# A written order, separate load places and GpSimd steps for the w_k products of an attention, RWKV-FFN and conv-FFN kernel

## Chip, core and metric

The kernel runs on one core of a Trainium2 chip. The metric is the device time of one execution in microseconds (us), lower is better. TensorE does the matrix products, VectorE and ScalarE the element-wise work, GpSimd (POOL in the profile) some of it, and SyncE (SP) starts most DMA transfers.

## What is computed

The output of a causal attention is the input of a token-mixing feed-forward layer, whose output is the input of a second feed-forward layer with a convolution of three taps. The part that changes is the first half of the middle layer, `k = max(xk @ w_k, 0)` and the first of the six column slices of `k*k @ w_v`.

```python
x = attention(q, k, v)                      # (2, 448, 768), causal softmax, 12 heads of 64
x_prev = x shifted by one token
xk = mu_k * x + (1 - mu_k) * x_prev         # (896 tokens, 768)
xr = mu_r * x + (1 - mu_r) * x_prev
k = np.maximum(xk @ w_k, 0.0)               # w_k: 768 x 1024
v = k * k @ w_v                             # w_v: 1024 x 768
r = 1.0 / (1.0 + np.exp(-(xr @ w_r)))
x = r * v
h = np.maximum(x @ w_in, 0.0); gate = sigmoid(conv3(h, conv_w))
return (h * gate) @ w_out
```

## The kernel before

**Products.** Every matrix product runs in three passes: each float32 operand is kept as a high part H and a remainder L (both in the type that TensorE takes at full rate), and `mm3` issues H*H, H*L, L*H. For `xk @ w_k` the kernel uses a 2x2 scheme with seven block products instead of eight. Its eight columns of 128 are taken in four groups g = 0 to 3, each with one 128-column slice of the left half of w_k and one of the right half. Group g needs seven weight operands of 128x384: A11, A12, A22 are pieces of the two slices, S1 to S4 are sums and differences of pieces (step D). Each operand gets a step H (a copy to the product type) and a step L (the remainder). A product P1 to P7 is nine matmuls of 448 columns. P1, P6, P7, P4 add into one PSUM bank (A), P5 and P3 into another (B), P2 has its own (D), with evictions between: P1, P5, P6 are copied out (cp), P2, P3, P7 are added to a copy (ad), and the result goes through max with 0 (re), square (sq), H (kh) and L (kl) to become `k2[f]` for one half of the tokens. P4 ends its bank with re, sq, kh, kl. `k2[f]` is then the right operand of the w_v slices (`pv0` to `pv5` in the profile, 48 matmuls each).

**Weights.** Weights come as 8-byte floats. A load puts them in a place of 8-byte words; `narrow` makes 4-byte floats of them in place, step a on ScalarE and step e on VectorE. Two places (`raws`) are used in turn by all slices, so a load waits until all readers of the slice before the last are done. Prepared operands lie in four places (`whls`), of two operands each for w_k.

**Order.** The attention part before (`ORDER`, up to 122 us in the profile) and the last part (`LATE`) follow lists written out in the kernel: one token is one step, and each engine does its steps in the list's order. Between them, from `START = 3` on, the loops over `PORD` (products) and `WORDER` (operands) give program order, and the framework's scheduler sets each engine's order. Each engine works through its queue in order, so a step that waits holds all behind it. All VectorE and ScalarE steps of `k_split`, `k_out` and `k_evict` are on those two engines; GpSimd has nothing between 120 us and 280 us but one clearing of 0.1 us.

Of the kernel before, what the change touches and what calls it, by code (L numbers as in the profile page):

```python
# [22 lines left out]
def kernel(  # L23
# [629 lines left out]
    PORD = [(x, 0) for x in ("P1", "P2", "P5", "P6", "P3", "P7")]  # L653
    for g_ in range(1, KH):
        PORD += [(x, g_) for x in ("P1", "P5", "P2", "P6")] + [("P4", g_ - 1), ("P3", g_), ("P7", g_)]
    WORDER = [(n, 0) for n in ("A11", "A12", "S1", "S2", "S4", "S3", "A22")]
    WORDER += [(n, g_) for g_ in range(1, KH) for n in ("A11", "S1", "A12", "S2", "S4", "S3", "A22")]
    place = {w: n for n, w in enumerate(WORDER)}
    k_raw, w_pairs, w_done, k_bank, k_begun = {}, {}, {}, {}, set()

    def w_value(g_, n):
# [14 lines left out]
            split_l(eng or "v", t[:, 1], x, t[:, 0])  # L676

    def w_operand(g_, n):
        i, j = divmod(place[n, g_], 2)
        if i not in w_pairs:  # L680
            w_pairs[i] = whls.get(f"q{i}", f"wq{i}")[:, :, :2 * WT].rearrange("p a (b c) -> p a b c", b=2)
        return w_pairs[i][:, :, j]

    def k_product(x, g_):
        g_ = int(g_)
        a, b, acc = USES[x]
        more = (acc, g_) in k_begun
        if not more:
            k_begun.add((acc, g_))
            k_bank[acc, g_] = bank(f"k{acc}{g_}", 1) if pinned[0] else next_bank(f"k{acc}{g_}")  # L690
# [8 lines left out]
        n = place[a, g_]  # L699
        w_done[n // 2] = w_done.get(n // 2, 0) + 1  # L700
        if w_done[n // 2] == 2:
            whls.put(f"q{n // 2}")
# [93 lines left out]

    HALF = [slice(0, 512), slice(512, NT)]

    def token_mm(name, w, x, late_):
# [3 lines left out]
        order = [(c, b) for b in range(B) for c in KORD[:-2]] + [(c, b) for b in range(B) for c in KORD[-2:]] if late_ else [
            (c, b) for b in range(B) for c in range(n)]
        for i, (c, b) in enumerate(order):
            if k_tail and i == B * (n - 2):
                k_tail.pop()()
                for y in range(2):
                    whls.put(f"v{y}")
            products(out_[b], w, x, HALF[b], n, c, order[-1][0])  # L810
# [5 lines left out]
    def k_convert(g_):  # L816
        for r in range(2):
            if not loaded:
                load_next()
            raw, n, name = loaded.pop(0)[1]  # L820
            k_raw[g_, r] = raw
            convert(raw, n, name)

    def k_split(g_, n):
        if n[0] == "S":
            w_step(g_, n, "D", "")
        w_step(g_, n, "H", "s")
        w_step(g_, n, "L", "v")

    def k_out(a, f, b, relu):  # L830
        if k2[f] is None:
            k2[f] = big(f"Y{KHOME[f]}", f"k2_{f}")
        if relu:
            nc.scalar.activation(a, a, AF.Relu)
        nc.scalar.activation(a, a, AF.Square)
        split_h("s", k2[f][:, 0, TOK[b]], a)
        split_l("v", k2[f][:, 1, TOK[b]], a, k2[f][:, 0, TOK[b]])
# [428 lines left out]
```

## Time and profile before

| | us |
|---|---|
| median of three timed runs (lowest to highest) | 351.71 (351.44 to 353.42) |
| profiled execution, its own time | 353.43 |
| its span, first to last instruction | 351.6 |
| PE busy in the span | 338.7 |
| DVE (VectorE) busy | 275.2 |
| ACT (ScalarE) busy | 249.0 |
| POOL (GpSimd) busy | 93.1 |

TensorE's granted clock is 1.00 of full speed (2.4 GHz) over the whole span. A busy engine is executing an instruction; time between instructions is put down to what released the next one.

### The profile page before, as it was taken

What the parts mean: (1) busy time and instruction counts of PE and PEld (TensorE: products, weight loads), DVE (VectorE), ACT (ScalarE), POOL (GpSimd) and SP (SyncE); (2) the same over time, 40 slices, a digit from 0 to 9 for tenths busy, and PEclk for the clock granted to TensorE, in tenths of its full rate; (3) what the DMA queues carried; (4) which work ended last, traced back from release to release, by engine and by line L of the source; (5) the groups of instructions that cost most, each with busy time, mean ns of one, the idle gap of its engine ahead of it and who ended that gap; (6) DMA issues with size and microseconds to landing.
All of it is one profiled execution on the core that took longest, in us unless ns stands there. A gap on an engine that the chain in (4) does not pass through costs nothing.

```text
span 351.6 us, 7133 instructions
## 1 busy us (share of the span) xinstructions
PE 338.7 (96%) x2644; PEld 302.7 (86%) x2644; DVE 275.2 (78%) x604; ACT 249.0 (71%) x545; POOL 93.1 (26%) x153
## 2 busy tenths in 40 slices
PE   8989999999999999998979999999999999999995
PEld 7677788988898999897858999998988999999995
DVE  3999989999999949769566987446686889898731
ACT  2999989999880068889897875334657878766501
POOL 8376978866410400000000000000000000367110
PEclk9999999999999999999999999999999999999999
DMA  6658577251150052241793765222505200379623
GB/s 170 147 125 208 131 215 181 69 168 46 58 168 2 0 179 93 87 125 56 277 349 124 258 246 180 89 89 91 179 15 167 89 0 3 67 134 213 126 90 136
DMA packets 60095, 45.28 MB, mean 129 GB/s; under 512 B 31624, under 2 KB 58668, under 8 KB 60060
## 3 DMA queue, kind: packets, MB, share of 16 engines
q1 hardware_dynamic: 55916, 39.31, 36.7%
q0 software_dynamic: 3408, 5.33, 7.7%
q8 instruction: 21, 0.34, 0.4%
q10 hardware_dynamic: 736, 0.18, 0.2%
q14 instruction: 14, 0.11, 0.1%
HBM read 38.12 MB, written 2.75 MB: 116 GB/s over the span
## 4 chain that ended last, share of the span: by engine, by line
PE 67%; ACT 13%; DVE 11%; DMA 5%; issue 2%; SPq 1%; DVEq 0%; ACTq 0%
PE pv L69 16%; PE A L69 7%; PE po L425 5%; ACT p L377 5%; PE pr L69 4%; PE B L69 4%; PE c L69 2%; PE s L355 2%; ACT wt L138 2%; PE D L69 2%; DVE mixed L637 2%; DVE wq L94 2%; DMA wk6raw<-in_moe_w_k_dram 2%; PE W L600 2%; DVE xopX L94 1%
## 5 line engine op out<-in xcount | busy, mean ns | idle before, releaser
L1089 POOL DMA_DIRECT2D s<-g x12 | 12.6, 1169 | 131.4 <-ACT st L90 124.8
L377 ACT ACTIVATE p<-e,st 128x192 f32<-128x192 f32 (+6 forms) x84 | 42.4, 522 | 2.3 <-DVE st L368 2.2
L75 POOL TENSOR_SCALAR p<-p,st 128x256 f32<-128x256 f32 (+6 forms) x74 | 36.5, 512 | 16.3 <-DVE st L385 10.0
L368 DVE CUSTOM_DVE_ANT_0 e<-s,mask 128x192 f32<-128x192 f32 (+6 forms) x84 | 31.4, 413 | 1.8 <-PE s L355 1.6
L1006 DVE SCALAR_TENSOR_TENSOR cv<-hT,cw,cv 128x448 f32<-128x448 f32 x32 | 21.5, 680 | 6.7 <-ACT cv L1003 6.6
L425 PE MATMUL po<-pt,v 128*64 128x128 f32 (+4 forms) x384 | 24.1, 277 | 0.2 <-ACT pt L82 0.2
L425 PEld LDWEIGHTS po<-pt,v 128*64 128x64 f32 x384 | 20.2, 137 | 3.5 <-ACT pt L82 0.6
L355 PE MATMUL s<-kT,qT 64*64 64x192 f32 (+6 forms) x336 | 22.3, 385 | 0.6 <-ACT kT L82 0.5
L355 PEld LDWEIGHTS s<-kT,qT 64*64 64x64 f32 x336 | 14.7, 132 | 6.5 <-ACT kT L82 0.9
L377 ACT ACTIVATION_READ_ACCUMULATOR p<-e,st 128x1 f32 x84 | 17.7, 211 | 0.0
L69 PE MATMUL kA<-xopX,wq 128*128 128x448 f32 x72 | 16.7, 367 | 0.7 <-DVE aP L854 0.7
L846 ACT ACTIVATE aP<-kB 128x448 f32<-128x448 f32 x4 | 2.2, 543 | 21.4 <-PE kB L69 21.4
L69 PEld LDWEIGHTS kA<-xopX,wq 128*128 128x128 f32 x72 | 13.4, 188 | 2.2 <-DVE aP L854 1.1
L963 POOL MEMSET hT<- 128x6 f32 x1 | 0.1, 107 | 54.1 <-PE kA L69 54.1
L1012 DVE TENSOR_TENSOR cv<-cv,hT 128x448 f32<-128x448 f32 x16 | 9.9, 621 | 4.4 <-ACT cv L1010 4.3
L1010 ACT ACTIVATE cv<-cv 128x448 f32<-128x448 f32 x16 | 9.1, 568 | 5.6 <-DVE cv L1006 5.6
L69 PE MATMUL pv<-k,wv0hl 128*128 128x512 f32 (+1 forms) x48 | 10.2, 368 | 2.5 <-ACT wv0hl L90 2.2
L94 DVE TENSOR_TENSOR k<-aP,k 128x448 fp32r<-128x448 f32 x16 | 9.9, 620 | 3.5 <-ACT k L90 3.3
L94 POOL TENSOR_TENSOR xr<-m,xr 128x448 fp32r<-128x448 f32 x10 | 12.0, 1204 | 1.8 <-ACT xr L90 1.2
L69 PEld LDWEIGHTS pv<-k,wv0hl 128*128 128x128 f32 x48 | 8.6, 188 | 4.2 <-ACT wv0hl L90 2.6
L1201 ACT ACTIVATE o<-A 128x384 f32<-128x384 f32 x3 | 1.5, 491 | 14.5 <-PE A L69 14.5
L1003 ACT ACTIVATE cv<-hT,cw 128x448 f32<-128x448 f32 x16 | 10.7, 667 | 1.0 <-DVE g L94 0.8
(446 smaller groups left out, 1085.6 us busy)
## 6 DMA issues: line engine op xcount, KB each, us to landing
rqk<-in_q_dram SPq DMA_DIRECT2D x23, 112.0 KB, 3.2
v<-in_v_dram SPq DMA_DIRECT2D x24, 96.0 KB, 3.5
s<-g POOLq DMA_DIRECT2D x12, 192.0 KB, 3.8
rqk<-in_k_dram SPq DMA_DIRECT2D x16, 112.0 KB, 3.0
wo6raw<-g POOLq DMA_DIRECT2D x8, 192.0 KB, 4.7
wv0raw<-in_moe_w_v_dram SPq DMA_DIRECT2D x1, 1022.0 KB, 4.9
wv1raw<-in_moe_w_v_dram SPq DMA_DIRECT2D x1, 1022.0 KB, 7.2
wv2raw<-in_moe_w_v_dram SPq DMA_DIRECT2D x1, 1022.0 KB
```

Source lines behind the costliest of these rows:

```text
L69: nc.tensor.matmul(ps_out, x, y, start=first and i == 0, stop=last and i == 2, skip_group_check=more,)
L75: nc.gpsimd.tensor_scalar(out_, in_, s, 1.0, ALU.mult, ALU.mult)
L94: e.tensor_tensor(out_, x, f32(h), ALU.subtract)
L355: nc.tensor.matmul(held[self.name(f"s{f}")][1][h, o:z], qT[r, i * LO:(i + 1) * LO], kT[r, :(i + 1) * LO], start=True, stop=True,)
L368: nc.vector.tensor_tensor_reduce(t[:, :w], used(self.name(f"s{f}"))[:, o:z], mask[:, S - w:], -SCALE, 3e38, ALU.add, ALU.min, self.st[:, 0 ...
L377: nc.scalar.activation(p[:, :w], self.s[i][:, :w], AF.Exp, bias=self.st[:, 0, i:i + 1], scale=-1.0, accum_out=self.st[:, 1, i:i + 1],)
L425: nc.tensor.matmul(self.T["po"][j * D:(j + 1) * D, 1 + i * LO - z:1 + (i + n) * LO], self.v[:, kc, j], self.T["pt"][:, a - z:a + n * LO], ...
L1003: nc.scalar.activation(a, x[:, 0:S], AF.Copy, scale=cw[:, f:f + 1])
L1006: nc.vector.scalar_tensor_tensor(a, x[:, j:S + j], cw[:, j * NF + f:j * NF + f + 1], a, ALU.mult, ALU.add)
L1010: nc.scalar.activation(a, a, AF.Sigmoid)
L1012: (nc.gpsimd if eng == "p" else nc.vector).tensor_tensor(a, a, hc, ALU.mult)
L1089: nc.gpsimd.dma_start(out=dst, in_=f32(x), accum_op=ALU.add)
```

## The change

1. The loops over `PORD` and `WORDER` go. A list `PK` takes their place, in the manner of `ORDER`: it fixes the order of the seven products' remaining runs, of all operand steps, evictions and of the first w_v slice (tokens V0 to V7, one for each `k2[f]`) on TensorE, ScalarE, VectorE and GpSimd, and that of the loads.
2. The raw slices of group 2 (wk2, wk6) load into the places of `k2[2]` and `k2[6]`, outputs that are written later. The two `raws` places then serve groups 1 and 3 and the w_v slices.
3. The max with 0 of P2, P3 and P7 moves from ScalarE to GpSimd. So do step D of S3 and S4 and step L of A22 in groups 1 to 3, from VectorE.
4. The copies out of PSUM get two more places (five in all), and the last A22 operand a place of its own.
5. The last P4 stands after V0 and V4 in the list. The number of products and matmuls is the same.

A token reads `step.group:kind/engine`: `P2.1:ad` is the eviction `ad` of P2 in group 1, `S3.1:D/p` the difference S3 of group 1 on GpSimd, `k2.1:L` the load of group 2's second slice (`a` and `e` narrow it), `v0:h` a step of the first w_v slice, `P3.1` alone the product.

```diff
-    START = 3
-    w_next = len(WORDER) // KH
-    for n, (x, g_) in enumerate(PORD):
-        if n >= START:
-            k_product(x, str(g_))
-        k_evict(x, g_)
...
-            k_split(h, a)
-            w_next += 1
...
+    a_free = list(mslots.free) + list(
+        act.tile([P, 2, S], F32, tag="T2", name="aT").rearrange("p b s -> b p s")
+    )
+    a_at, k_top, v_c, v_hl, pv0 = {}, {}, {}, {}, []
+
+    def k_step(g_, r, s):
+        if s == "L":
+            tag = f"Y{KHOME[g_ + r * KH]}"
+            x = home(tag).tile([P, NC * P], I64, tag=tag, name=f"wk{g_ + r * KH}raw") if g_ == 2 else None
+            k_raw[g_, r] = load(*plan.pop(0), x)[0]
+            return
...
+        elif s == "re":
+            if x == "P4":
+                nc.scalar.activation(a, y, AF.Relu)
+            else:
+                nc.gpsimd.tensor_scalar(a, a, 0.0, 1.0, ALU.max, ALU.mult)
...
+    PK = """
+        k1.0:L P5.0:cp k1.1:L k2.0:L k2.1:L P1.0:cp P6.0 k1.0:a P2.0:ad P2.0:re/p k1.0:e P3.0 P6.0:cp P2.0:sq
+        A11.1:H k1.1:a P7.0 P3.0:ad A11.1:L A12.1:H P3.0:re/p k1.1:e P2.0:kh P1.1 k2.0:a A12.1:L S3.1:D/p S1.1:D
+        P3.0:sq P7.0:ad A22.1:H P2.1 S2.1:D S1.1:H P7.0:re/p k2.0:e P1.1:cp S4.1:D/p S2.1:H S1.1:L P4.0 P7.0:sq
+        S2.1:L S3.1:H A22.1:L/p P2.1:ad A11.2:H k3.0:L P3.0:kh S3.1:L P5.1 P2.1:re/p S4.1:H A11.2:L P4.0:re
+        P2.0:kl A12.2:H S4.1:L k2.1:a P3.0:kl P6.1 k3.1:L A12.2:L P5.1:cp k2.1:e P2.1:sq P3.1 P7.0:kh P6.1:cp
+        S1.2:D S3.2:D/p P4.0:sq P7.0:kl P2.1:kh S2.2:D P7.1 S1.2:H P3.1:ad P4.0:kh S4.2:D/p P2.1:kl S2.2:H
+        S1.2:L k3.0:a P1.2 P3.1:re/p S2.2:L P7.1:ad k3.1:a k3.0:e P7.1:re/p P2.2 P3.1:sq P4.0:kl S4.2:H k3.1:e
+        P1.2:cp P7.1:sq P4.1 S4.2:L S3.2:H S3.3:D/p P2.2:ad A11.3:H P3.1:kh S3.2:L P2.2:re/p A12.3:H A11.3:L
+        P5.2 P4.1:re S1.3:D P7.1:kh A12.3:L A22.2:H P3.1:kl P6.2 P2.2:sq P7.1:kl A22.2:L/p P5.2:cp S2.3:D
+        P4.1:sq S1.3:H S4.3:D/p P3.2 P6.2:cp S1.3:L S2.3:H P2.2:kh S2.3:L P4.1:kh P7.2 P3.2:ad S4.3:H v0:L
+        P2.2:kl A22.3:H P3.2:re/p S4.3:L P1.3 S3.3:H A22.3:L/p P4.1:kl P3.2:sq P7.2:ad S3.3:L P3.2:kh P7.2:re/p
+        P2.3 P1.3:cp v1:L P3.2:kl P7.2:sq P4.2 P7.2:kh P2.3:ad P7.2:kl v0:a P2.3:re/p P5.3 P4.2:re v0:e P2.3:sq
+        P4.2:sq P6.3 P5.3:cp v0:h P3.3 P2.3:kh v0:l P6.3:cp P4.2:kh v1:a P2.3:kl P7.3 P3.3:ad P4.2:kl P3.3:re/p
+        v1:e V0 P3.3:sq P7.3:ad V4 v1:h P7.3:re/p P4.3 P3.3:kh v1:l P7.3:sq P7.3:kh P3.3:kl V1 P4.3:re P7.3:kl
+        V5 P4.3:sq P4.3:kh V2 P4.3:kl V6 V3 V7
+    """
...
+            else:
+                w_step(g_, n, s, eng or "vs"[s == "H"])
+
+    pinned[0] = True
+    with tc.manual_schedule(engines={ET.PE, ET.Activation, ET.DVE, ET.Pool}):
+        for token in PK.split():
+            issue_k(token)
+    pinned[0] = False
...
-        for t, pv in token_mm(f"pv{e}", w, k2, e == 0):
+        for t, pv in token_mm(f"pv{e}", w, k2) if e else zip(HALF, pv0):
```

**GpSimd, behind its last step of the attention part.** Before, the step on xopH is followed by the clearing of hT:

```order
L94 TENSOR_TENSOR xopH<-mixed_114,xopH 128x448
L963 MEMSET hT 128x3x2
L1089 DMA s_0_3189<-g_3287 128x384
```

Now 21 steps stand between; these are the first ten (L863 is the max with 0 on a copied product aP or aT, L667 the difference S3 or S4 on raw weights, L94 the step L of A22):

```order
L94 TENSOR_TENSOR xopH<-mixed_114,xopH 128x448
L863 TENSOR_SCALAR aP_2297<-aP_2297 128x448
L863 TENSOR_SCALAR aP_2321<-aP_2321 128x448
L667 TENSOR_TENSOR wk5raw<-wk1raw,wk5raw 128x384
L863 TENSOR_SCALAR aP_2289<-aP_2289 128x448
L667 TENSOR_TENSOR wk5raw<-wk1raw 128x384
L94 TENSOR_TENSOR wq_2337<-wk5raw,wq_2337 128x384
L863 TENSOR_SCALAR aT<-aT 128x448
L667 TENSOR_TENSOR wk6raw<-wk2raw,wk6raw 128x384
L667 TENSOR_TENSOR wk6raw<-wk2raw 128x384
L863 TENSOR_SCALAR aP_2446<-aP_2446 128x448
```

Twelve of the 21 are maxima, six differences, three steps L.

**SyncE, the loads of w_k and w_v.** Before (in brackets what each waits for; DMAHW are the transfers that used the same counter before):

```order
L161 DMA wk5raw<-in_moe_w_k_dram 128x6x511 [waits DMAHW0_49,DMAHW2_49,DVE_49,Activation_49]
L161 DMA wk2raw<-in_moe_w_k_dram 128x6x511 [waits DMAHW3_49,DMAHW1_49,DVE_49]
L161 DMA wk6raw<-in_moe_w_k_dram 128x6x511 [waits DMAHW4_49,DMAHW2_49,DVE_49]
L161 DMA wk3raw<-in_moe_w_k_dram 128x6x511 [waits DMAHW3_49,DVE_49]
L161 DMA wk7raw<-in_moe_w_k_dram 128x6x511 [waits DMAHW4_49,DVE_49]
```

And now:

```order
L161 DMA wk5raw<-in_moe_w_k_dram 128x6x511 [waits DMAHW0_49,DMAHW2_49,DVE_49,Activation_49]
L161 DMA wk2raw<-in_moe_w_k_dram 128x6x511 [waits DMAHW3_49,PE_49]
L161 DMA wk6raw<-in_moe_w_k_dram 128x6x511 [waits DMAHW4_49,PE_49]
L161 DMA wk3raw<-in_moe_w_k_dram 128x6x511 [waits DMAHW1_49,DVE_49,Pool_49]
L161 DMA wk7raw<-in_moe_w_k_dram 128x6x511 [waits DMAHW2_49,DVE_49,Pool_49]
```

The order is the same. The loads of group 2 no longer wait for VectorE's reading of group 1 but for TensorE's last product with xr, whose places they take; those of group 3 wait for group 1's readers on VectorE and GpSimd.

**VectorE, the same steps at the start of the part.** Now, from the narrowing of group 1's first slice to that of group 2's first (L858 is `ad`, which reads PSUM; L140 is step e; wq are operands):

```order
L140 SCALAR_TENSOR_TENSOR wk1raw_2287<-wk1raw_2287,wt_0_70 128x768
L858 TENSOR_TENSOR aP60_2321<-kB0_2246,aP60_2321 128x448
L94 TENSOR_TENSOR wq3_2257<-wk1raw_2287,wq3_2257 128x384
L140 SCALAR_TENSOR_TENSOR wk5raw_2291<-wk5raw_2291,wt_1_71 128x768
L94 TENSOR_TENSOR wq4_2337<-wk1raw_2287,wq4_2337 128x384
L667 TENSOR_TENSOR wk1raw_2287<-wk5raw_2291 128x384
L858 TENSOR_TENSOR aP50_2289<-kA0_2262,aP50_2289 128x448
L667 TENSOR_TENSOR wk1raw_2287<-wk1raw_2287 128x384
L140 SCALAR_TENSOR_TENSOR wk2raw_2293<-wk2raw_2293,wt_0_70 128x768
```

All but the two L858 read two tensors in SBUF. Before, the narrowing of wk2raw stood behind all of group 1's operand steps and three evictions more.

## Rows read from the trace of the kernel before

**Rows 1.** Busy us of the engines in stretches (PE, PEld, DVE, ACT, POOL, clock, DMA, GB/s).
```profile
120.00:180.00 60.00, 55.28 (x266) 49.07 (x264) 44.13 (x79) 48.07 (x89) 0.11 (x1) 1.00 0.44 149
180.00:340.00 160.00, 160.00 (x828) 147.99 (x829) 118.31 (x194) 104.49 (x185) 18.06 (x22) 1.00 0.45 124
```

**Rows 2.** Waits of TensorE, 110 to 200 us (total us, times, longest).
```profile
PE pv L69 <- ACT wv0hl L90: 2.2, 1, 2.2
PE kA L69 <- ACT wq L90: 1.5, 2, 0.9
PE kA L69 <- DVE aP L854: 0.7, 1, 0.7
PE pv L69 <- DVE wv0hl L94: 0.3, 1, 0.3
```

**Rows 3.** Timeline of TensorE, 120 to 200 us (start, us, instruction).
```profile
125.51 1.38 PE L69 MATMUL kD<-xopX,wq 128*128 128x448 f32 x6
...
143.75 1.38 PE L69 MATMUL kA<-xopX,wq 128*128 128x448 f32 x6
...
178.50 1.08 PE L69 MATMUL pv<-k,wv0hl 128*128 128x512 f32 x4 [2.21 <-ACT wv0hl L90]
...
188.90 9.83 PE L69 MATMUL pv<-k,wv1hl 128*128 128x512 f32 x48
198.57 1.78 PE L69 MATMUL pv<-k,wv2hl 128*128 128x512 f32 x7
```

**Rows 4.** The chain that ended last, 100 to 200 us (start, us).
```profile
138.69 5.54 DMA wk6raw<-in_moe_w_k_dram
...
176.23 1.24 ACT wt L138
```

**Rows 5.** Timeline of SyncE's DMA issues, 95 to 215 us.
```profile
124.30 0.37 SPq L161 DMA_DIRECT2D wk5raw<-in_moe_w_k_dram  x1
136.75 0.37 SPq L161 DMA_DIRECT2D wk2raw<-in_moe_w_k_dram  x1
...
168.04 0.37 SPq L161 DMA_DIRECT2D wv0raw<-in_moe_w_v_dram  x1
```

**Rows 6.** Timeline of VectorE in the changed part.
```profile
133.24 0.55 DVE L670 TENSOR_TENSOR wk5raw<-wk1raw,wk5raw 128x384 f32<-128x384 f32 x1
133.71 0.61 DVE L854 TENSOR_TENSOR aP<-kB,aP 128x448 f32<-128x448 f32 x1
134.24 0.55 DVE L670 TENSOR_TENSOR wk1raw<-wk1raw 128x384 f32<-128x384 f32 x1
...
145.37 0.96 DVE L140 SCALAR_TENSOR_TENSOR wk6raw<-wk6raw,wt 128x768 int32<-128x768 int32 x1 [0.73 <-ACT wt L138]
```

**Rows 7.** Timeline of VectorE, 84 to 112 us.
```profile
84.15 1.15 DVE L94 TENSOR_TENSOR wr0hl<-wr0raw,wr0hl 128x768 fp32r<-128x768 f32 x1
...
100.26 0.99 DVE L94 TENSOR_TENSOR xopX<-mixed,xopX 128x448 fp32r<-128x448 f32 x1
```

**Rows 8.** Timeline of GpSimd, 60 to 125 us.
```profile
84.58 1.73 POOL L94 TENSOR_TENSOR xr<-m,xr 128x448 fp32r<-128x448 f32 x1
...
99.57 1.20 POOL L94 TENSOR_TENSOR xopX<-mixed,xopX 128x448 fp32r<-128x448 f32 x1 [5.80 <-ACT xopX L90]
```

**Rows 9.** Line 94, by tile (ns minimum/median/maximum).
```profile
L94 POOL TENSOR_TENSOR xr<-m,xr x10: 1137/1145/1727, 33.3 to 88.9; 128x448 fp32r<-128x448 f32 x10
L94 DVE TENSOR_TENSOR xopX<-mixed,xopX x10: 608/610/991, 90.9 to 112.0; 128x448 fp32r<-128x448 f32 x10
```

**Rows 10.** GpSimd by line and shape (busy us, mean ns).
```profile
L75 POOL TENSOR_SCALAR p<-p,st 128x448 f32<-128x448 f32 x10 | 7.1, 708 | 2.2 <-DVE st L385 2.2
...
L86 POOL TENSOR_SCALAR xr<-m 128x448 fp32r<-128x448 f32 x8 | 4.5, 563 | 0.0
...
L94 POOL TENSOR_TENSOR wr2hl<-wr2raw,wr2hl 128x768 fp32r<-128x768 f32 x1 | 1.9, 1865 | 0.5 <-DVE wr2hl L88 0.5
...
L94 POOL TENSOR_TENSOR wq<-wk0raw,wq 128x384 fp32r<-128x384 f32 x1 | 1.2, 1223 | 15.1 <-issue 15.1
```

More of the change, by code (lines that the diff above doesn't have):

```diff
@@ L652 @@
             "P3": ("S4", "B22", "B"), "P7": ("S3", "T3", "A"), "P4": ("A22", "T4", "A")}
[L653 to L658, printed above, removed]
+    place = {n: i for i, n in enumerate(("A11", "A12", "S1", "S2", "S4", "S3", "A22"))}
+    LONE = ("A22", KH - 1)
+    w_place = {}
     k_raw, w_pairs, w_done, k_bank, k_begun = {}, {}, {}, {}, set()
@@ L678, in w_operand @@
     def w_operand(g_, n):
[L679 to L682, printed above, removed]
+        if (n, g_) not in w_place:
+            if (n, g_) == LONE:
+                w_place[n, g_] = None, act.tile([P, 2, WT], F32R, tag="T5", name="wqT")
+            else:
+                i, j = divmod(place[n] if g_ == 0 else len(w_place), 2)
+                if i not in w_pairs:
+                    w_pairs[i] = whls.get(f"q{i}", f"wq{i}")[:, :, :2 * WT].rearrange("p a (b c) -> p a b c", b=2)
+                w_place[n, g_] = i, w_pairs[i][:, :, j]
+        return w_place[n, g_][1]
     def k_product(x, g_):
@@ L689, in k_product @@
             k_begun.add((acc, g_))
[L690 removed]
+            k_bank[acc, g_] = bank(f"k{acc}{g_}", 1) if g_ == 0 else next_bank(f"k{acc}{g_}")
         w = w_operand(g_, a)
@@ L698, in k_product @@
             )
[L699 to L702, printed above, removed]
+        i = w_place[a, g_][0]
+        w_done[i] = w_done.get(i, 0) + 1
+        if w_done[i] == 2:
+            whls.put(f"q{i}")
     xr_done = [0] * NE
@@ L797, with token_mm @@
     HALF = [slice(0, 512), slice(512, NT)]
-    def token_mm(name, w, x, late_):
+    def token_mm(name, w, x):
         n = len(x)
         out_ = [next_bank(f"{name}_{b}")[:, :t.stop - t.start] for b, t in enumerate(HALF)]
[L803 to L810, printed above, removed]
+        for b, t in enumerate(HALF):
+            for c in range(n):
+                products(out_[b], w, x, t, n, c)
         return list(zip(HALF, out_))
@@ L814 @@
     k2 = [None] * NF
[L816 to L837, printed above, removed]
@@ L889 @@
-    k_tail = [lambda: k_next("P4", KH - 1)]
+    a_free = list(mslots.free) + list(
[8 more added lines that the diff above has]
+            return
+        raw = k_raw[g_, r][:, :NC * P]
+        if s == "a":
+            k_top[g_, r] = tops.turn("")[:, :NC * P]
+        narrow(s, within(raw), raw, k_top[g_, r])
@@ new lines, in v_step @@
+    def v_step(i, s):
+        if s == "L":
+            v_c[i] = load(*plan.pop(0))
+            return
+        raw, n, name = v_c[i]
+        c = within(raw)[:, :n]
+        if s == "a":
+            k_top[i] = tops.turn("")[:, :n]
+        if s in "ae":
+            narrow(s, c, raw[:, :n], k_top[i])
+        elif s == "h":
+            v_hl[i] = whls.get(f"v{i}", f"{name}hl")[:, :, :n]
+            split_h("s", v_hl[i][:, 0], c)
+        else:
+            split_l("v", v_hl[i][:, 1], c, v_hl[i][:, 0])
@@ new lines, with issue_k @@
+    """
+    def issue_k(token):
+        what, _, eng = token.partition("/")
+        what, _, s = what.partition(":")
+        if what[0] == "V":
+            if not pv0:
+                pv0.extend(next_bank(f"pv0_{b}")[:, :t.stop - t.start] for b, t in enumerate(HALF))
+            f = int(what[1])
+            for b, t in enumerate(HALF):
+                products(pv0[b], [v_hl[0]], k2, t, 0, f, NF - 1)
+        elif what[0] == "v":
+            v_step(int(what[1]), s)
+        else:
+            n, g_ = what.split(".")
+            g_ = int(g_)
+            if n[0] == "k":
+                k_step(int(n[1]), g_, s)
+            elif not s:
+                k_product(n, g_)
+            elif n[0] == "P":
+                k_evict(n, g_, s, eng)
+            else:
+                w_step(g_, n, s, eng or "vs"[s == "H"])
@@ L891 @@
+    pinned[0] = True
[3 more added lines that the diff above has]
+    pinned[0] = False
+    mslots.free[:] = [t for t in a_free if isinstance(t, str)]
+    for key in list(whls.held):
+        whls.put(key)
+    ready.extend([v_hl[i]] for i in range(2))
     x2 = []
```

61 lines of the change are left out of this document (23 added, 38 removed).

## Prediction

> **What bounds the kernel now.** I read the stretches first: from 180 to 340 us TensorE is busy for all 160 us, in the stretch of the change, 120 to 180 us, for 55.3 of 60 [rows 1]. So TensorE sets the end, and a microsecond that it wins or loses before 180 us should reach the end undiminished: nothing later waits for a clock of its own. The list of TensorE's waits gives 4.7 us there, in five pieces [rows 2]; the timeline says what they cost in all. From the start of P2 in group 0 to that of the second w_v slice it takes 188.90 - 125.51 = 63.39 us [rows 3]. Its work there is 26 products (28 less P5 and P1 of group 0) and the 48 matmuls of the first w_v slice. Ten products in a row without a wait took 143.75 - 125.51 = 18.24 us, so 1.824 each; the 48 matmuls of the second slice took 198.57 - 188.90 = 9.67 us. Work: 26 x 1.824 + 9.67 = 57.1 us. Loss: **6.3 us**, the recorded waits and 1.6 us more, which I put to restarts and to waits for an L part inside a product. That is all that the change can win.
>
> What is late, by the chain of waits: a transfer of group 2's second slice, on the chain for 5.5 us, with its narrowing behind it (group 3's is the same again), and, at the last and largest wait of 2.2 us, w_v's narrowing: 1.24 us on ScalarE for the second slice stand in its queue between the first slice's steps [rows 4, 2].
>
> **The change, part by part.** *Loads.* wk2raw is issued at 136.75 us, because its place is read until then; wk5raw goes at 124.30 [rows 5]. Now wk2 and wk6 wait only for TensorE's last xr product, about 122 us, and follow wk5. Priced like wk6, whose transfer stood on the chain for 5.5 us, each behind the one ahead, they land near 131 and 134 us at the latest, before any of group 2's steps is due. Group 1's places then serve group 3: its loads start when group 1's steps are read out, near 140 us, some 12 us earlier than now. That removes the transfers from TensorE's path. wv0 goes at 168.04 us now [rows 5]; it will go when group 3's steps are done, near 160 us, and its four steps stand apart from those of the second slice. The first w_v products (V0, V4) need only `k2[0]` and `k2[4]`; the last P4 covers the wait for others. Neither costs anything.
>
> *List.* Product order within a bank leaves a product of another bank between an eviction and the next use of its bank. With the durations of now, no product would wait: I find at least 0.6 us of slack at each of them. So without a side cost the change wins all 6.3 us.
>
> *GpSimd.* Here is the side cost. 12 maxima and 9 two-input steps move to it. ScalarE is relieved, and VectorE of 9 x 0.47 us; but the trace shows that a GpSimd step and a VectorE step that reads two SBUF tensors do not run side by side. At 84.58 us a GpSimd step of 448 took 1.73 us where the quickest took 1.137; it ran, then, from 85.17, and the VectorE step beside it, begun at 84.15, ended at 85.30 [rows 7, 8, 9]. Seen from the other side, VectorE's step at 100.26 us took 0.99 us instead of 0.61, so it ran from 100.64; the GpSimd step ahead of it ended at 100.77 [rows 7, 8, 9]. In both cases the one behind ran 0.13 us before the recorded end of the one ahead. In the k part nearly all of VectorE's work is of this kind; only `ad`, with one operand from PSUM, should be exempt, since the VectorE steps on PSUM in the attention part keep their length beside GpSimd.
>
> The sum goes over the tightest stretch: from the end of P3 in group 0 (131.1 us, three products after 125.51 and a little) to the `ad` of P7 in group 2 (`P7.2:ad`), which P4 in group 2 (P4.2), twenty products after 125.51 us, needs by 125.51 + 20 x 1.824 = 162.0 us to start without a wait. That is 30.9 us. In the list VectorE has there 23 steps D or L of 384, 9 steps kl and 8 `ad` of 448, 5 steps e of 768. From start to start a step of 384 takes 0.47, one of 448 0.53 us, and the record of 0.96 for step e less the same overlap of 0.08 gives 0.88 [rows 6]. So 23 x 0.47 + 17 x 0.53 + 5 x 0.88 = 24.2 us. GpSimd has 9 two-input steps of 384 and 7 maxima of 448 there. The trace shows a one-input step of 448 with constants at 0.563 [rows 10]. For two inputs of 384 I go along the line from 1.137 at 448 [rows 9] to 1.865 at 768 [rows 10], 2.275 ns an element: 0.99 us. Less 0.13 each, they hold VectorE off for 9 x 0.86 + 7 x 0.43 = 10.8 us, unless they lie beside an `ad`. Bounds: each of the 8 `ad` hides its full 0.53, then 24.2 + 6.5 = 30.7 us and no stall; none hides anything, then 35.0 us, 4.1 over. Of VectorE's 24.2 us 4.2 are exempt, a sixth to a fifth, so by chance 1.9 us are hidden and 8.9 fall on VectorE: 33.1 us. Walking both queues step by step in the listed order with these durations gives 9.1, and with it 2.5 us over; five or six short waits (P3.1, P4.1, P3.2, P7.2, P4.2) carry it, with some 0.1 us for each restart. I take **3.0 us**. After P4.2 the load eases, since no operands are left to prepare, and no more is lost.
>
> *Added waits.* The sq of P2, P3 and P7 now wait on ScalarE for a maximum on GpSimd, with H steps queued behind them; by the walk the longest such wait is 1.7 us (P7.2), and the products that need those H steps stand more than 2 us later, so I price it at nothing; with the cover gone it is 1.7. The scheduler also puts the narrowing of the third w_v slice on ScalarE ahead of the sq of the last P7, and its load goes only after the last P3's end (SyncE has a w_out load that waits for that in front): near 179 us it frees ScalarE, some 2.5 us late. V7 waits for that, but 15 to 23 matmuls of the second slice now stand ahead of it on TensorE, 3.0 us or more at 0.2 each. That hides it.
>
> Sum: 6.3 - 3.0 = 3.3 us won. Against the profiled execution's own 353.43 us (span 351.6 and 1.8 around it) that is 350.1; the median of the three timed runs, 351.71, lies 1.7 us below that execution, so 351.71 - 3.3 = **348.4 us** for the median.
>
> The Trainium skill, "SBUF — State Buffer", section "SBUF: two separate sides", calls the port pair that VectorE and GpSimd share an exclusive lock, held for the whole instruction, the loser fully blocked. The two pairs of rows agree that the loser is blocked, but show the pair free 0.13 us before the record ends. With whole records, 9 x 0.99 + 7 x 0.563 = 12.9 us held, 0.82 of it on VectorE, and 0.05 us at each of 16 hand-overs back, I get 24.2 + 10.5 + 0.8 = 35.5, 4.6 us over, and 350.2 us for the median instead of 348.4.
>
> **Rivals.** *A, the pair of engines costs nothing.* If the maxima and differences fall beside `ad` steps and into VectorE's pauses, the full 6.3 us are won: 345.4 us. For it speaks the lower bound above; against it that VectorE has no pauses left in that stretch by my walk. Chance 0.2.
>
> *B, it costs nearly all.* Whole-instruction holding gives 4.6 us over, as worked out, so 350.2. If beside that the new steps are as slow as their slowest kin, 1.22 us for two inputs of 384 and 0.71 for a maximum of 448 [rows 10], 16.0 us are held, 13.1 fall on VectorE, and 37.3 + 0.8 is 7.2 over: 352.6, no gain. Both numbers of the slow kin have reasons that may not apply (another VectorE step ahead; a factor from memory), so I put the case at 350 to 352. Against the first the 0.13 us. The Trainium skill's "GPSIMD Engine Reference", section 4.1, advises VectorE for such two-input steps, as about half as fast on GpSimd; 0.99 against 0.55 us here agrees. Chance 0.22.
>
> *C, slower.* No row shows a GpSimd step that waits while VectorE has several two-tensor steps in a row. If VectorE keeps the pair through such a run, GpSimd waits to the next `ad`: a run between two of them is (24.2 - 4.2) / 8 = 2.5 us, so 1.25 on average, and 16 such waits put 20 us on GpSimd's own 10.8: 30.8, as much as the stretch has. S3, S4 and A22 gate products, so GpSimd would then be the bound. It decides from 1.25 + (6.3 + 1.8) / 16 = 1.8 us a wait on: then more is lost than won, above 353.5 us. Chance 0.06.
>
> *D, the list is not what runs.* If a load of group 2 came no earlier, P1.2 would wait as now. The order of the queues speaks against it, with the wait for TensorE in place of that for VectorE. I give it 0.02, near 351.
>
> **Numbers.** My forecast has 0.5, its own range 347.0 to 350.0. A measurement of this kernel can tell about 0.5%, 1.8 us, from no change: its runs shown spread by 0.56%. Faster by over 0.5% is below 349.95: A and nearly all of the forecast, 0.69. Within 0.5%: B, D and a rest, 0.25. Slower: C, 0.06. The range of 8 in 10 reaches from A's end, 345.2, to 351.7 in B.
>
> **What would show it.** In the new trace: wk2 and wk6 issued near 125 us and landed before 135; wv0 issued near 160; no wait of TensorE for ScalarE's wq or wv steps at the starts of groups 2 and 3; GpSimd steps of 384 lengthened to well over 0.99 and VectorE's two-tensor steps of 384 to well over 0.55 in places, together by about 9 us up to P4.2; TensorE's waits at P4 and P3 of groups 1 and 2, for `ad` and `cp`, 3 us together; the start of the second w_v slice's matmuls followed by no gap up to 340 us. Wrong it would be if VectorE's lengthened steps sum to under 5 or over 12 us, if ScalarE waits long for a maximum and holds H steps behind it, or if TensorE gets a wait after 190 us that it does not have now.

## The result and the profile after

The changed kernel takes 349.56 us (median of seven runs, 348.45 to 350.42), the kernel before 353.42 in the runs beside it (seven, 351.44 to 354.28). The ratio is 0.989, interval 0.986 to 0.992: faster by 1.1%, inside the predicted range of 347.0 to 350.0 us and 1.2 us above the forecast of 348.4. The forecast started from 351.71 us for the kernel before, which took 1.7 us more here, so the medians give 3.9 us won where 3.3 were forecast. The profiled execution took 350.42 us, its span 348.4.

The two stretches, as in [rows 1] (after the stretch and its length stand busy time and count of TensorE, its weight loads, VectorE, ScalarE and GpSimd, then TensorE's granted clock):

```profile
120.00:180.00 60.00, 57.83 (x280) 51.79 (x279) 48.60 (x71) 41.27 (x74) 34.86 (x22) 1.00 0.47 153
180.00:340.00 160.00, 160.00 (x832) 148.23 (x831) 117.02 (x193) 105.00 (x187) 19.05 (x23) 1.00 0.44 125
```

TensorE still fills all of 180 to 340 us, so it sets the end as before. All that is won lies ahead of 180 us, where it was busy for 55.28 us and now is for 57.83. GpSimd, idle there before, is busy for 34.86 us; at the prediction's prices its 21 steps would take 9 x 0.99 + 12 x 0.563 = 15.7. TensorE's waits from 110 to 340 us, to compare with [rows 2] (us in total, times, longest):

```profile
PE kB L69 <- ACT aT L856: 1.4, 1, 1.4
PE kB L69 <- ACT aP L856: 0.8, 1, 0.8
```

None is left for a weight operand or for w_v. Both new ones are of one kind: P3 of group 2 (P3.2, at 157.75 us) and of group 1 (P3.1, at 143.12) wait for `cp`, ScalarE's copy of P5 out of the bank that P3 writes next. TensorE's timeline, as [rows 3], at the start of P2 in group 0, at P3.1, at P3.2 and at the start of the third w_v slice:

```profile
125.72 0.57 PE L69 MATMUL kD<-xopX,wq 128*128 128x448 f32 x2
...
143.12 1.48 PE L69 MATMUL kB<-xopX,wq 128*128 128x448 f32 x6 [0.81 <-ACT aP L856]
...
157.75 1.49 PE L69 MATMUL kB<-xopX,wq 128*128 128x448 f32 x6 [1.35 <-ACT aT L856]
...
195.85 1.31 PE L69 MATMUL pv<-k,wv2hl 128*128 128x512 f32 x5
```

The first two w_v slices now overlap on TensorE, so I measure all kernels to the third: 26 products of 1.824 us and 2 x 9.67 us of w_v matmuls are 66.76 us of work. Before, 198.57 - 125.51 = 73.06 us: a loss of 6.3 [rows 3]. Now 195.85 - 125.72 = 70.13: a loss of **3.4 us**. The profile gives 2.9 us won, the prediction's sum 3.3. P3.1 stands nine products behind P2 of group 0 and starts 143.12 - 125.72 - 9 x 1.824 = 1.0 us late; P3.2, seven products on, starts 157.75 - 125.72 - 16 x 1.824 = 2.85 us late. So most of the 3.4 us is lost by then.

SyncE's timeline, to compare with [rows 5]:

```profile
124.49 0.37 SPq L161 DMA_DIRECT2D wk5raw<-in_moe_w_k_dram  x1
124.95 0.49 SPq L161 DMA_DIRECT2D wk2raw<-in_moe_w_k_dram  x1
125.55 0.49 SPq L161 DMA_DIRECT2D wk6raw<-in_moe_w_k_dram  x1
139.72 0.37 SPq L161 DMA_DIRECT2D wk3raw<-in_moe_w_k_dram  x1
...
160.87 0.37 SPq L161 DMA_DIRECT2D wv0raw<-in_moe_w_v_dram  x1
```

wk6 goes 13 us earlier [rows 4], wv0 7 us, and wk2 lands 7.1 us after its issue, at 132.1 us. That part went as foreseen. GpSimd's groups by shape from 120 to 180 us (count, busy us, mean ns):

```profile
L863 POOL TENSOR_SCALAR aP<-aP 128x448 f32<-128x448 f32 x9 | 18.4, 2039 | 18.7 <-DVE aP L858 18.7
L863 POOL TENSOR_SCALAR aT<-aT 128x448 f32<-128x448 f32 x3 | 5.7, 1913 | 0.5 <-DVE aT L858 0.5
L667 POOL TENSOR_TENSOR wk6raw<-wk2raw,wk6raw 128x384 f32<-128x384 f32 x1 | 1.6, 1570 | 2.2 <-DVE wk6raw L140 2.2
...
L667 POOL TENSOR_TENSOR wk6raw<-wk2raw 128x384 f32<-128x384 f32 x1 | 0.8, 828 | 1.0 <-DVE wk2raw L667 1.0
```

The maximum takes 2.0 us, not 0.563. The prediction took that price from a GpSimd step of the same shape which multiplies [rows 10]. The two-input steps take 0.83 us undisturbed (forecast 0.99) and up to 1.57. ScalarE's waits between 128 and 165 us are mostly for that maximum:

```profile
ACT aP L865 <- POOL aP L863: 4.7, 5, 1.3
ACT aP L856 <- PE kA L69: 1.7, 1, 1.7
ACT wq L90 <- DVE wk2raw L667: 1.0, 1, 1.0
```

VectorE pays too. From 131 to 162 us its steps on SBUF tensors (L, kl, D and e) are busy for 18.32 us (25 at line 94), 4.31 (6 at line 667) and 5.11 (5 at line 140). In the kernel without GpSimd steps (below) the same kinds come to 16.36 us for 31, 6.48 for 12 and 4.77 for 5. At these lengths the 36 steps in the changed kernel would take 13.2 + 3.2 + 4.8 = 21.2 us; they take 18.32 + 4.31 + 5.11 = 27.7, so they are lengthened by **6.5 us**.

So two accounts stand for the 3.4 us still lost. Q: the maximum of 2.0 us makes ScalarE's queue late, and with it `cp`. ScalarE's timeline ahead of P3.2 fits it: ScalarE works without a pause from the end of its wait for a maximum to the `cp` that P3.2 waits for:

```profile
152.98 0.58 ACT L865 ACTIVATE aP<-aP 128x448 f32<-128x448 f32 x1 [1.25 <-POOL aP L863]
...
157.18 0.52 ACT L856 ACTIVATE aT<-kB 128x448 f32<-128x448 f32 x1
```

X (for the two-input steps) and P (for the maxima): GpSimd's steps shut VectorE off from the ports, and what VectorE delivers late makes ScalarE, and `cp` behind it, late.

### The profile page after: what moved, and what is told of

The parts are those of the page before. It is cut to its first block, busy times and chain, and to the rows that moved or that the text cites. A ratio compares the mean times of both kernels' runs of the same rounds, so it can differ in the third digit from the quotient of the medians.

```text
span 348.4 us, 7146 instructions
## 1 busy us (share of the span) xinstructions
PE 338.4 (97%) x2644; PEld 303.1 (87%) x2644; DVE 278.2 (80%) x595; ACT 242.6 (70%) x533; POOL 127.9 (37%) x174
## 4 chain that ended last, share of the span: by engine, by line
PE 71%; DVE 11%; ACT 9%; issue 3%; POOL 2%; DMA 2%; SPq 1%; DVEq 0%; POOLq 0%; ACTq 0%
PE pv L69 17%; PE A L69 7%; ACT p L377 5%; PE po L425 5%; PE pr L69 4%; PE B L69 4%; PE kA L69 3%; PE c L69 2%; PE s L355 2%; POOL aP L863 2%; DVE wq L94 2%; PE D L69 2%; DVE mixed L637 2%; PE kB L69 2%; DVE xopX L94 2%
## 5 line engine op out<-in xcount | busy, mean ns | idle before, releaser
L863 POOL TENSOR_SCALAR aP<-aP 128x448 f32<-128x448 f32 x9 | 18.4, 2039 | 18.7 <-DVE aP L858 18.7
L69 PE MATMUL kA<-xopX,wq 128*128 128x448 f32 x66 | 15.4, 368 | 0.0
L856 ACT ACTIVATE aP<-kB 128x448 f32<-128x448 f32 x2 | 1.1, 540 | 19.6 <-PE kB L69 19.6
L69 PE MATMUL kB<-xopX,wq 128*128 128x448 f32 x48 | 11.4, 372 | 2.2 <-ACT aT L856 1.4
L69 PEld LDWEIGHTS kA<-xopX,wq 128*128 128x128 f32 x66 | 12.2, 188 | 1.4 <-DVE aP L858 0.3
L94 POOL TENSOR_TENSOR xr<-m,xr 128x448 fp32r<-128x448 f32 x10 | 12.0, 1203 | 1.8 <-ACT xr L90 1.2
L69 PEld LDWEIGHTS kB<-xopX,wq 128*128 128x128 f32 x48 | 8.8, 188 | 3.9 <-ACT aT L856 2.0
L94 DVE TENSOR_TENSOR x<-xv,x 128x512 fp32r<-128x512 f32 (+1 forms) x12 | 7.3, 618 | 5.9 <-ACT x L90 5.9
```

Source lines behind the costliest of these rows:

```text
L69: nc.tensor.matmul(ps_out, x, y, start=first and i == 0, stop=last and i == 2, skip_group_check=more,)
L94: e.tensor_tensor(out_, x, f32(h), ALU.subtract)
L863: nc.gpsimd.tensor_scalar(a, a, 0.0, 1.0, ALU.max, ALU.mult)
```

## The experiments

The loss below is always that from P2 of group 0 to the third w_v slice, less 66.76 us; "longer" is the sum of VectorE's lengthening as above, over 31 us from 5.3 us behind the start of P2. The kernel before took 354.49, 353.47, 353.36 and 354.24 us in the four groups of runs. The loss leaves out the attention part ahead of P2 of group 0. No edit touches that part, yet it lasts from 123.4 to 127.7 us in these profiles, and 127.7 and 123.6 in the two profiles of the kernel without GpSimd steps. So where kernels differ by 1 to 2 us in time, the loss is the better measure.

| kernel | group | us | ratio to before | loss | longer |
|---|---|---|---|---|---|
| maxima on ScalarE | 1 | 347.54 | 0.982 (0.978 to 0.986) | 2.2 | 6.3 |
| two-input steps on VectorE | 1 | 348.89 | 0.985 (0.981 to 0.988) | 2.1 | 1.6 |
| no GpSimd steps | 1 | 347.06 | 0.981 (0.977 to 0.984) | 0.9 | 0.0 |
| before, loads only | 1 | 351.93 | 0.993 (0.990 to 0.997) | 6.4 | |
| changed, again | 2 | 349.48 | 0.990 (0.985 to 0.995) | 3.4 | 6.5 |
| multiplication for maximum | 2 | 350.62 | 0.990 (0.986 to 0.994) | 3.3 | 7.7 |
| spare two-input steps | 2 | 350.39 | 0.991 (0.987 to 0.995) | 4.5 | 4.8 |
| maximum with one operation | 2 | 347.88 | 0.984 (0.979 to 0.989) | 2.7 | 6.9 |
| list without load places | 3 | 362.73 | 1.027 (1.022 to 1.031) | 16.0 | |
| no GpSimd steps, cp first | 3 | 347.66 | 0.983 (0.979 to 0.987) | 1.0 | 0.0 |
| spare maxima | 4 | 348.05 | 0.981 (0.978 to 0.985) | 2.6 | 1.1 |
| no GpSimd steps, again | 4 | 346.32 | 0.977 (0.973 to 0.982) | 0.6 | 0.0 |

**One half of GpSimd's work at a time.** Maxima on ScalarE:

```diff
-                nc.gpsimd.tensor_scalar(a, a, 0.0, 1.0, ALU.max, ALU.mult)
+                nc.scalar.activation(a, a, AF.Relu)
```

> The changed kernel with the 12 maxima of P2, P3 and P7 on ScalarE again; the list, the load places and the nine two-input steps on GpSimd stay. Theory Q (what is left of TensorE's loss, 3.4 us between P2 of group 0 and the second w_v slice, comes from ScalarE, whose sq waits for maxima that take 2.0 us on GpSimd and holds the copies cp behind it): ScalarE gets 12 x 0.5 = 6 us but loses its waits; TensorE's waits of 1.4 and 0.8 us at P3.2 and P3.1 go, loss under 1.5 us, time 347 to 348. Theory X (the loss comes from VectorE, lengthened beside GpSimd's two-input steps): these stay, VectorE wins only the 0.36 us beside each maximum, the loss stays at 2.5 to 3.5 us, time 349 to 350. Theory S (ScalarE needs the relief): ScalarE's queue gets too full, loss over 4 us, time above 350.5.

Two-input steps on VectorE (the token of S3, S4 and A22 loses its /p in groups 1 to 3; the kernel without GpSimd steps has both edits):

```diff
-S3.1:D/p S1.1:D
+S3.1:D S1.1:D
...
-S2.1:L S3.1:H A22.1:L/p P2.1:ad
+S2.1:L S3.1:H A22.1:L P2.1:ad
```

> The changed kernel with the differences S3, S4 and step L of A22 on VectorE again; the maxima stay on GpSimd. Theory Q: ScalarE's waits for the maxima stay, so the loss stays near 3.4 us, time 349 to 350. Theory X: VectorE gets 9 x 0.47 = 4.2 us and is rid of some 4.7 us of lengthening beside the two-input steps; TensorE's waits shrink by 1 to 2 us, time 347.5 to 348.5. If VectorE needs the relief after all, waits for ad and L steps appear, time above 350.5.

> The changed kernel with all 21 GpSimd steps back on ScalarE and VectorE: what is left of the change is the list, the load places and the two more copy places. Theories Q and X together: VectorE has 28 us of work in the tightest 31 us and no lengthened step, ScalarE no wait for GpSimd; the loss falls under 1.5 us, time 346.5 to 347.5, better than the change. If the relief by GpSimd is worth more than its waits cost: loss of 4 us or more, time above 350.

Each half costs: without the maxima the loss falls from 3.4 to 2.2, without the two-input steps to 2.1, without both to 0.9 and, taken a second time, 0.6. Q foresaw about 3.4 for the second edit, X 2.5 to 3.5 for the first: neither is the whole. Without the maxima the wait at P3.2 is gone, although VectorE is lengthened by 6.3 us, hardly less than the 6.5 before; so what the maxima cost in the changed kernel does not show in that sum. About 0.5 us of the 2.2 left there follow no recorded wait: the products from P7.1 (143.51 us) to P7.3 (169.55) start every 1.86 us instead of 1.824, and no run shows why. Nobody needed the relief: all 21 steps back on VectorE and ScalarE give the smallest loss (by its time alone, 0.981, that kernel is not told apart from the one with the maxima on ScalarE, 0.982). TensorE's waits from 110 to 340 us in its second profile, and the stretch to 180 us:

```profile
PE kB L69 <- ACT aP L856: 0.2, 1, 0.2
```

```profile
120.00:180.00 60.00, 59.83 (x295) 54.69 (x294) 44.94 (x78) 53.14 (x95) 0.11 (x1) 1.00 0.56 188
```

How a two-input step on GpSimd reaches TensorE is seen in the kernel with the maxima on ScalarE, ahead of P3.1, in the timelines of GpSimd, VectorE and ScalarE (start, length; in brackets the wait before):

```profile
134.48 1.47 POOL L667 TENSOR_TENSOR wk5raw<-wk1raw 128x384 f32<-128x384 f32 x1 [1.50 <-DVE wk1raw L667]
135.91 1.35 POOL L94 TENSOR_TENSOR wq<-wk5raw,wq 128x384 fp32r<-128x384 f32 x1
```

```profile
135.19 2.49 DVE L94 TENSOR_TENSOR wq<-wk1raw,wq 128x384 fp32r<-128x384 f32 x2
137.60 0.61 DVE L858 TENSOR_TENSOR aT<-kD,aT 128x448 f32<-128x448 f32 x1
```

```profile
138.25 0.58 ACT L863 ACTIVATE aT<-aT 128x448 f32<-128x448 f32 x1 [1.01 <-DVE aT L858]
...
140.99 0.51 ACT L856 ACTIVATE aP<-kB 128x448 f32<-128x448 f32 x1
```

Two VectorE steps L take 2.49 us together instead of 1.0, beside two GpSimd steps in a row. The eviction `ad` of P2 behind them ends late, ScalarE waits 1.01 us for it, and `cp` of P5.1, five steps on in its queue, starts at 140.99: P3.1 waits 1.2 us. The wait is put down to ScalarE; its cause is two engines away.

**Steps that nobody waits for.** Eight two-input steps added to the kernel without GpSimd steps (those of A22 in groups 1 and 2 likewise):

```diff
             nc.vector.tensor_tensor(x, w_value(g_, y), w_value(g_, z), o)
+            if g_ and n in ("S3", "S4"):
+                nc.gpsimd.tensor_tensor(spare(), w_value(g_, y), w_value(g_, z), o)
```

> The kernel without GpSimd steps in the k part, with eight two-input steps of 384 added on GpSimd beside it (the operands of S3, S4 and of A22 in groups 1 and 2 read a second time, the result in a place that nobody reads). No engine waits for them. Theory X (two-input steps cost by lengthening VectorE's): VectorE is lengthened by 3 to 6 us in all, with all its own work still on it, the loss rises from 0.9 to 2 to 4 us, time 348 to 350. Theory L (the change pays for them because S3, S4 and A22 come late from GpSimd): VectorE may be lengthened, but the loss stays under 1.3 us, time 346.5 to 347.5.

TensorE's waits in it:

```profile
PE kB L69 <- ACT aP L867: 1.2, 1, 1.2
PE kB L69 <- DVE wq L94: 1.1, 1, 1.1
PE kB L69 <- ACT aT L867: 1.1, 1, 1.1
```

X holds, L falls: VectorE, ScalarE, TensorE and SyncE have no recorded wait for GpSimd in this part, VectorE is 4.8 us longer, and the loss is 3.6 to 3.9 us above that of the same kernel without them. The loss of 4.5 and the time of 350.39 us lie a little above X's 2 to 4 and 348 to 350. VectorE still has its own copies of these steps here, so that is more than the 1.2 to 1.5 us which the two-input steps cost in the changed kernel. The same for seven maxima:

```diff
             split_l("v", k2[f][:, 1, TOK[b]], a, k2[f][:, 0, TOK[b]])
+            if x != "P4" and ("A22", KH - 1) not in w_place:
+                nc.gpsimd.tensor_scalar(spare[:, :S], f32(k2[f][:, 1, TOK[b]]), 0.0, 1.0, ALU.max, ALU.mult)
```

> The kernel without GpSimd steps in the k part, with seven maxima of 448 added on GpSimd (each reads a finished L part of k2 of groups 0 to 2 and writes where nobody reads); no engine waits for them. Theory Q (the maxima cost because ScalarE waits for them): VectorE's steps beside their starts are longer by 0.3 to 0.4 us, 1.5 to 2.8 us in all, but the loss stays under 1.0 us, time within 0.7 us of the kernel without GpSimd steps beside it. Theory P (they cost by what they hold of VectorE): the loss rises by 1 us or more, to that of the kernel with the maxima alone on GpSimd, 1.8 us, time 1 us or more above.

TensorE's waits in it:

```profile
PE kB L69 <- ACT aT L859: 0.7, 1, 0.7
PE kA L69 <- DVE aT L861: 0.4, 1, 0.4
PE kB L69 <- ACT aP L859: 0.2, 1, 0.2
```

VectorE is only 1.1 us longer, and P3.2, which did not wait in the kernel without GpSimd steps, waits 0.7 us. The 0.4 us is my own doing: a later ScalarE step waited 2.6 us for the last spare maximum, whose result lay in its place. So part of the 2.0 us above the loss of the kernel without them counts for nothing. But the wait at P3.2 comes ahead of that and speaks for P: maxima cost although nobody waits for them. From P2 of group 0 to P3.2 it takes 0.85 us more than without them (30.47 against 29.62), with only three of VectorE's steps lengthened on the way. In the kernel with the two-input steps on VectorE, where ScalarE waits for the maxima, the same stretch takes 31.07 us, 1.45 more. I estimate from these that more than half of what the maxima cost needs nobody to wait for them; different VectorE steps are hit in the two kernels, so the split is not shown. (The 1.8 us that the expectation gives for that kernel's loss stands as 2.1 in the table.)

**The maximum itself.** Multiplying by 1 in its place (the max of P2, P3 and P7 is left out), and the maximum written with one operation:

```diff
-                nc.gpsimd.tensor_scalar(a, a, 0.0, 1.0, ALU.max, ALU.mult)
+                nc.gpsimd.tensor_scalar(a, a, 1.0, 1.0, ALU.mult, ALU.mult)
...
+                nc.gpsimd.tensor_scalar(a, a, 0.0, None, ALU.max)
```

> The changed kernel, but the 12 GpSimd steps multiply by 1 instead of taking the maximum with 0 (the max of P2, P3 and P7 is left out; same tile, same shape, same queue). Theory Q (the 2.0 us of a maximum, through ScalarE's queue): the multiplication takes 0.56 us as it did elsewhere in the kernel before, ScalarE's waits for GpSimd shrink from 0.5 to 1.8 us each to under 0.3, the loss falls from 3.4 to about 2.2 us, as with the maxima on ScalarE; time 1.0 to 1.5 us below the changed kernel. Theory P (the maximum costs by holding the pair of ports, whatever its length): VectorE's steps beside these twelve stay 0.36 us longer, the loss stays at 3 to 3.5 us, time as the changed kernel.

> The changed kernel, with the GpSimd maximum written with one operation (max with 0) instead of two (max with 0, times 1). If the second operation made the step long: 0.5 to 1.2 us each and 1 us below the changed kernel; if it is the maximum itself: 1.9 to 2.1 us each and the changed kernel's time within 0.5 us.

GpSimd's larger group in each, the multiplication first:

```profile
L863 POOL TENSOR_SCALAR aP<-aP 128x448 f32<-128x448 f32 x9 | 8.1, 896 | 22.1 <-DVE aP L858 22.1
```

```profile
L863 POOL TENSOR_SCALAR aP<-aP 128x448 f32<-128x448 f32 x9 | 14.9, 1660 | 19.8 <-DVE aP L858 19.8
```

With steps less than half as long ScalarE's waits for GpSimd between 128 and 165 us shrink from 4.7 to 1.0 us, and the loss stays at 3.3: P's forecast. It is no clean test, since the wait at P3.2 does fall, from 1.4 to 0.3 us, as Q has it, and others come in its place. The multiplication, 0.56 us at its quickest, takes 0.896 on average, and VectorE is 1.2 us longer than in the changed kernel: the two hold each other up, and ScalarE waits for VectorE instead. The maximum with one operation takes 1.5 to 1.7 us on average, between the two forecasts, with 0.7 us less loss. ScalarE's waits for GpSimd only shrink from 4.7 to 3.3 us over the same stretch, so the 0.7 us is no upper bound on what they cost. Its 347.88 us against 349.48 is more than its loss explains; 1.0 us of that lies in the attention part of its profile (123.79 us to P2 of group 0 against 124.77).

**Loads and list apart.** The kernel before with the load places alone:

```diff
-                load_next()
-                load_next()
+                for r in range(2):
+                    tag = f"Y{KHOME[h + r * KH]}"
+                    load_next(home(tag).tile([P, NC * P], I64, tag=tag, name=f"wk{h + r * KH}raw") if h == 2 else None)
```

> The kernel before with one part of the change alone: the raw slices of group 2 load into the places of k2[2] and k2[6]; order from the scheduler, no step on GpSimd. If the late loads were most of the loss of 6.3 us: wk2 and wk6 land before 135 us, the two waits of 1.5 us for ScalarE's wq at group starts go, w_v loads come earlier too, time 3 us or more below the kernel before. If the order of the list is what gives: TensorE waits at other places instead, time within 1 us of the kernel before.

SyncE's timeline and TensorE's waits in it:

```profile
118.44 0.37 SPq L161 DMA_DIRECT2D wk2raw<-in_moe_w_k_dram  x1
120.49 0.37 SPq L161 DMA_DIRECT2D wk6raw<-in_moe_w_k_dram  x1
121.04 0.41 SPq L161 DMA_DIRECT2D wk1raw<-in_moe_w_k_dram  x1
```

```profile
PE kA L69 <- ACT wq L90: 2.5, 1, 2.5
PE kB L69 <- DVE wq L94: 0.4, 1, 0.4
```

The waits at groups 2 and 3 are gone, as the first theory had it; the time, 2.6 us below the kernel before, lies between the two forecasts. But the scheduler puts wk2 and wk6 ahead of wk1 on SyncE; wk1, needed first, shares the transfer engines with them and stands on the chain for 8.2 us, 4.4 in the changed kernel. Group 1 then starts with a wait of 2.5 us. The list sets the order of the loads too, so the two parts depend on each other. The other half:

```diff
-            x = home(tag).tile([P, NC * P], I64, tag=tag, name=f"wk{g_ + r * KH}raw") if g_ == 2 else None
+            x = home(tag).tile([P, NC * P], I64, tag=tag, name=f"wk{g_ + r * KH}raw") if False else None
...
-S1.2:L k3.0:a P1.2
...
+P4.0:kh P2.1:kl k2.0:a k2.0:e A11.2:H A11.2:L A12.2:H A12.2:L P1.2
```

> The list, but no load places and no GpSimd steps: the slices of group 2 load into the two shared places again, and the steps that need them are moved back in the list to where these loads can be there (groups 2 and 3). Theory O (the list's order alone gives the gain): loss under 2 us, time within 1 us of the kernel without GpSimd steps, 346.5 to 348. Theory P (it needs the places, since a load can go only when its place is read out): TensorE waits at P1, P2 or P5 of groups 2 and 3 behind a transfer, 3 to 7 us in all, time 349.5 to 353.5.

P holds in kind, with waits far over its price: TensorE waits 9.8 us, the largest 4.8 for a `cp` that stands behind the narrowing of wv0, whose load comes late in its turn. How much of that is the places and how much the moved steps, one list cannot tell: inconclusive on the size. Last, a token moved in the best kernel:

```diff
-k2.1:a P3.0:kl P6.1 k3.1:L A12.2:L P5.1:cp k2.1:e
+P3.0:kl P6.1 k3.1:L A12.2:L P5.1:cp k2.1:a k2.1:e
```

> The kernel without GpSimd steps (list and load places as changed), with one token moved: the copy of P5 in group 1 stands ahead of the narrowing of group 2's second slice on ScalarE. If that narrowing of 1.0 us in front of the copy is all that is left of the waits: TensorE's wait of 0.2 to 0.3 us at P3.1 goes, loss under 0.2 us, time 346.2 to 347.2, 1.9 to 2.2% below the kernel before. If another step is late behind it: a wait of the same size elsewhere, same time.

The wait at P3.1 goes and one of 0.5 us comes at P3.2: no gain. The controls:

> The changed kernel itself once more, as the measure for the others beside it. If the gain over the kernel before does not hang on the chip: ratio 0.986 to 0.992, time 348.5 to 350.5, and waits of TensorE for the copies at P3.1 and P3.2 again.

> The kernel without GpSimd steps once more, as the measure for the one beside it and as the best version so far: ratio to the kernel before 0.978 to 0.985, 346.5 to 347.5 us, loss under 1 us.

Both repeat. The best version is the list with its load places and nothing on GpSimd: 0.977 and 0.981 of the kernel before, against 0.989 and 0.990 of the changed one.

## Why the prediction was right

*The bound and what can be won.* TensorE sets the end, and 6.3 us were to be had. The kernel without GpSimd steps loses 0.6 to 0.9 us, so loads and list do win nearly all of it, as priced: some 28 us of work on VectorE (24.2 and nine steps of 0.47 more) fit into the 30.9 us that it has.

*The side cost.* Priced at 3.0 us, it measured 3.4 - 0.6 to 3.4 - 0.9, so 2.5 to 2.8 us. In kind the mechanism was right: GpSimd's steps hold up VectorE's two-input steps, and VectorE has little room for it. That the size fits is in part luck. VectorE's lengthening, forecast at 8.9 to 9.1 us up to P4.2 (and wrong under 5 or over 12), measured 6.5; with it the prediction's own sum gives 24.2 + 6.5 = 30.7 us, less than the 30.9 there are, and no loss. Losses came all the same, because TensorE does not wait for the whole of VectorE's queue: it waits at P3.1 and P3.2, far ahead of P4.2, for single copies that ScalarE makes late. Part of that lateness comes from ScalarE's waits for maxima, which were priced at nothing; how much, no run shows.

*Its terms.* The maximum was mis-sized in length, 2.0 us instead of 0.563, but hardly in how long it holds up a VectorE step. The timelines of VectorE and GpSimd in the changed kernel:

```profile
136.31 0.55 DVE L667 TENSOR_TENSOR wk1raw<-wk1raw 128x384 f32<-128x384 f32 x1
136.78 1.31 DVE L140 SCALAR_TENSOR_TENSOR wk2raw<-wk2raw,wt 128x768 int32<-128x768 int32 x1
```

```profile
136.47 1.95 POOL L863 TENSOR_SCALAR aP<-aP 128x448 f32<-128x448 f32 x1 [1.04 <-DVE aP L858]
```

The VectorE step that begins 0.3 us into the maximum takes 1.31 us instead of 0.95, 0.36 more; the prediction's 0.43 was close. The differences and A22's L were priced at a hold of 0.86 each; beside them single VectorE steps are 0.31 us (at 140.11 us) to 1.01 us (at 134.29 and 145.19) longer. The Trainium skill, "SBUF — State Buffer", section "SBUF: two separate sides", has the loser blocked for the whole instruction; the trace of the maximum does not agree, 0.36 of 1.95 us. By that rule, as an estimate from the measured 2.0 us, the seven maxima up to P4.2 alone would hold VectorE for 14 us.

*Places.* Five or six short waits were forecast at P3.1, P4.1, P3.2, P7.2 and P4.2. Of these only P3.1 and P3.2 have a recorded wait, and by the start of P3.2 2.85 of the 3.4 us are lost. What the walk left out is how little lies between `cp` of P5 and P3: ScalarE's queue delivers `cp` only when `ad` steps and maxima ahead of it are there.

*Added waits, priced at nothing.* The longest wait for a maximum before 165 us is 1.3 us, and 1.8 near 176 us, where no wait of TensorE follows; 1.7 was said. But there are five before 165 us, 4.7 us together, with H steps and `cp` queued behind them, which the prediction had named as a sign of being wrong. It had looked only at the H steps, and no product waits for one; P3.2 waits for the `cp`. What these waits cost apart from VectorE's lengthening stays open, as said above. Behind 190 us TensorE has no new wait, so the late narrowing of wv2 is covered as forecast.

*Rivals.* A (no cost) is what a kernel without GpSimd steps gives, not this one. B's whole-instruction lock and C's starved GpSimd did not happen: two-input steps on GpSimd last 1.57 us at most. D falls with SyncE's rows. B's first price is a slip, 351.71 - 6.3 + 4.6 = 350.0 us and not 350.2, and no row shows its 0.05 us for a hand-over; the measured 349.56 us alone is close to it, but the side cost that it needs is 4.6 us, and 2.5 to 2.8 were measured.

## What to carry to other kernels

Moving steps to an idle engine helps only if they do not shut out a busy one: add to the busy engine's queue how long the moved steps hold it up, and compare with the work that leaves it (here 6.5 us came for the 3.8 of eight steps that left). The sum of a queue does not say where a wait falls: follow the steps ahead of each copy too. When TensorE waits for a copy, follow that engine's queue back: the copy may be late because of a step two engines away. A transfer issued early takes bandwidth from the one that is needed first, so the order of issues belongs to the change.
